# A gated mix of attention and MLP in split fp32: engine queues filled from a build-time plan instead of hand-written delays

## The chip, the core and the metric

The kernel runs on one core of one Trainium2 chip. A core has a matrix engine (TensorE, PE in the profile, with its weight loads as PEld), three engines that work on elements (VectorE, DVE; ScalarE, ACT; GpSimd, POOL) and SyncE (SP), whose queue issues the transfers here. Each engine works through a queue of its own strictly in order; which instruction stands where in a queue is fixed when the kernel is built. The metric is the device time of one execution in microseconds, lower is better.

## The reference

For 2,048 positions of 448 features:

```python
g = sigmoid((x * gate_w).sum(-1))
# a: 16 heads of 28; query s sees the keys s, s-2, ... s-14 (8 of them, none below 0)
q, k, v = split(x @ wqkv)
a = softmax(q . k[s - 2 w] * 28**-0.5) . v[s - 2 w], then @ wo
h = relu(x @ w1 + b1) ** 2                      # 448 -> 1792
b = h @ w2 + b2                                 # 1792 -> 448
out = g * a + (1 - g) * b
```

Everything is fp32.

## The kernel before

**Products in parts.** TensorE multiplies numbers in a reduced form (fp32r). Each operand is therefore split: ScalarE copies its *high* part to fp32r, and a subtraction gives the *low* part, mostly on VectorE (`split_full`, lines 115 and 116). A product is three matmuls: high by high, high by low, low by high. In the names of the trace a final `h` or `l` tells the part (`w2ah`, `w2al`). The feature size 448 is three slices of 128 rows and one of 64; the matmuls use 64 rows each, in *pairs*: one on the upper and one on the lower half of the array, for two accumulators side by side (`side_by_side`, line 184). Each accumulator has to see both halves, so at mid-way the two change places. Before that a tiny instruction must be put between (`turn`, lines 192 and 194: a write to an unused column of the accumulator, on VectorE but for one case; in the MLP a `touch`, line 527, that rewrites a few weights in place on ScalarE).

**Layout.** Since the attention steps by two, positions are ordered by parity (`par`), and x comes in four chunks of 512 columns, two for each parity.

**Stages on TensorE.** Phase A computes q, k, v for the chunks in turn (`qkv_first`, line 253, then `qkv_two`); ScalarE evacuates the accumulators to stage tiles (`st`, line 203), which are stored to DRAM (`q_d`, `k_d`, `v_d`, line 209). From there the attention runs without TensorE, in eight units (parity by four head groups): q and k or v are loaded (lines 301, 302, 307), GpSimd multiplies (line 325 q by k, line 332 weights by v, eight of each in a unit, 128x896 each), VectorE reduces each product (lines 326 and 340), softmax lies between (lines 363 to 378), and the output is transposed (line 343) and stored (`o_d`, line 353). The product tiles have four buffers.

Meanwhile TensorE runs the MLP: 28 rounds, four chunks in the order 3, 0, 1, 2 with 14 tiles of 128 hidden features in pairs of two. In a round come `h_first` (12 pairs of matmuls of 512 columns), the touch, the first half of the second layer for the round before (`o_part`, 12 pairs of 448 columns, `b<-w2ah,h` and the like), a touch, `h_second` (9 pairs), and the second half (`o_all`, 12 pairs). For each of a round's two hidden tiles `mlp_ops` issues relu with bias (line 576), the square as high part (line 577), the square in place (line 578), all on ScalarE, and on VectorE the low part (line 575). Below, "low" without more is this one. `o_part` reads the high parts first and the lows from its third pair on.

At a chunk's end VectorE forms the gated sum (`bt`, line 762). The product of the attention's output with `wo` (`a`) is done in eight units: four for the first parity are slipped in between the MLP's rounds, four stand at the end. Their input is loaded (`ot`, lines 813 and 815) and split (lines 832 to 836).

Weights of the second layer come in two groups: `w2a`, in pieces of four and three tiles (`w2_piece`, lines 511 to 515; the low parts of the first on VectorE, of the second on GpSimd), and `w2b`, tile by tile (`w2_first`, line 903, two lows on GpSimd; the other five by way of a copy to an accumulator, line 897, on VectorE).

**What sets the order.** TensorE's stream is written out. The other engines' instructions are placed between its matmuls by hand: `advance` moves a clock of TensorE's time, `at`, `soon` and `when` put a function into a list with a time of that clock (constants `LO_DELAY`, `HL_DELAY`, `SPLIT_GAP`, `ATT_DELAY` and others), and the attention is a generator that is drawn on as its own clock falls behind:

```python
    def at(dt, fn):
        later.append((clock["pe"] + dt, fn))
...
        while clock["att"] < clock["pe"]:
            try:
                r = next(att)
```

Of the kernel before, what the change touches and what calls it, by code (L numbers as in the profile page):

```python
# [7 lines left out]
F32 = mybir.dt.float32  # L8
# [6 lines left out]
P = 128  # L15
# [15 lines left out]
MM512 = 227.0  # L31
MM448 = 203.0
QK_COST = 2300.0
AV_COST = 2000.0
SM_COST = 600.0
ATT_DELAY = 20000.0
LO_DELAY = 1500.0
HL_DELAY = 1800.0
SPLIT_GAP = 2000.0
ROW_GAP = 9200.0  # L40
OUT_DELAY = 2500.0
OUT_GAP = 3500.0
WO_DELAY = 4500.0
LOAD_DELAY = 1500.0
LAND_DELAY = 5000.0
OL_DELAY = 2500.0
KEY_DELAY = 10500.0
DEFER = 2
# [5 lines left out]
BT_BUFS = 8  # L54


@with_exitstack
def gated_mix_kernel(ctx: ExitStack, tc: tile.TileContext, xT, wqkv, w1, w2, wo, b1, b2, out):
# [5 lines left out]

# [6 lines left out]


# [6 lines left out]

    w1h = const.tile([P, 3, F], F32R, name="w1h")  # L80
    w1l = const.tile([P, 3, F], F32R, name="w1l")

# [12 lines left out]

# [15 lines left out]
    def now(fn):  # L111
        fn()

    def split_full(raw, hi, lo, soon=now):
        nc.scalar.activation(hi, raw, AF.Copy)
        soon(lambda: nc.vector.tensor_sub(lo, raw, f32(hi)))  # L116

    def split_x78(raw, x7, x8, soon=now):

        split_full(raw, x7, x8, soon)  # L120

    class X:

        def __init__(self, tiles):
            self.t = tiles
            self.h, self.l = [t[:, 0] for t in tiles[:3]], [t[:, 1] for t in tiles[:3]]
            self.x7, self.x8 = tiles[3][:, 0], tiles[3][:, 1]

# [3 lines left out]
    def x_split(raw, x, k):  # L134

        split_full(raw[:, k], x.t[k][:, 0], x.t[k][:, 1])

    def x_spill(c, x):
        for j in range(4):
            nc.sync.dma_start(x_d[c, j], f32(x.t[j]))  # L140
# [4 lines left out]

# [5 lines left out]

# [7 lines left out]
    stage = {}  # L159

# [3 lines left out]
    def block(b):  # L164

        o = (0, NP, NP + D)[b]
        return slice(o, o + ncols(b))

    class Acc:


        def __init__(self, tag, name, n, todo=21):
            self.pt, self.n, self.todo, self.rows = ps(tag, name), n, todo, None
            self.all = todo

    def side_by_side(*todo):


        assert len(todo[0]) == len(todo[1])
        for pair in zip(*todo):  # L180
            for r, (acc, a, w) in enumerate(pair):
# [3 lines left out]
                acc.todo, acc.rows = acc.todo - 1, r  # L185

    def turn(one, two):


        for acc in (one, two) if one is not two else (one,):  # L190
            if one is two:
                nc.scalar.activation(acc.pt[0:1, 511:512], none, AF.Copy)
            else:
                nc.vector.memset(acc.pt[0:1, 511:512], 0.0)  # L194
            acc.rows = None

    def qkv_evacuate(pt, c, tl, b):
        par, t = c // 2, (c % 2) * 4 + tl
        first = (b, t // 2) not in stage
        if first:  # L200
            stage[b, t // 2] = xap.tile([P, G, 2, C], F32, tag="stage", name=f"st{c}_{tl}_{b}", bufs=ST_BUFS)
        st = stage[b, t // 2]
        nc.scalar.activation(st[:, :, t % 2], pt[:, :D].rearrange("p (g c) -> p g c", g=G), AF.Copy)  # L203
        if not first:
# [4 lines left out]
            nc.sync.dma_start(dd.rearrange("p g s c -> p g (s c)"), st.rearrange("p g s c -> p g (s c)"))  # L209
        if b == 0:  # L210
            nc.scalar.activation(zt[:, par, t:t + 1], pt[:, D:D + 1], AF.Copy)

    def full(x, acc, tl, b, ks=range(3)):
        sl, n = slice(tl * P, tl * P + P), block(b)
        r = []
        for k in ks:
            r += [(acc, x.h[k][:, sl], wqh[:, k, n]), (acc, x.h[k][:, sl], wql[:, k, n]),
                  (acc, x.l[k][:, sl], wqh[:, k, n])]
        return r

    def last(x, acc, tl, b):

# [3 lines left out]
        return [(acc, x.x7[:, sl], h), (acc, x.x7[:, sl], l), (acc, x.x8[:, sl], h)]  # L226
# [4 lines left out]
    def run(c, todo, steps):  # L231


        a = 0
        for e, done, *turns in steps:
            side_by_side(todo[0][a:e], todo[1][a:e])
            while a < e:
                advance(min(12, e - a) * MM448)
                a = min(a + 12, e)
            for t in turns:  # L240
                t() if callable(t) else turn(*t)
            for b, tl, acc in done:
                assert acc.todo == 0
                qkv_evacuate(acc.pt, c, tl, b)

    def qkv_first(x):

        four = range(4)
        q = accs(0, 0, four, "bbbb")
        for k in range(3):  # L250
            for i in four:
                for j, (acc, a, w) in enumerate(full(x, q[i], i, 0, (k,))):
                    nc.tensor.matmul(acc.pt[:, :NQ], a, w, start=k == j == 0, stop=False)  # L253
            advance(12 * MM448)
# [19 lines left out]

# [12 lines left out]
    o_t = {}  # L287
    st_ = {"spilled": -1, "att": -1}
# [9 lines left out]
    def att_load_qk(par, g):  # L298
        q = attp.tile([P, NS, C], F32, tag="q", name=f"q{par}{g}")
# [773 lines left out]
```

## Time and profile before

| | us |
|---|---|
| median of 3 runs | 425.17 (424.88, 425.17, 425.71) |
| span of the profiled execution | 423.9, 9,324 instructions; 1.3 below the median |
| PE busy | 411.2 (97%), 3,844 matmuls |
| VectorE, ScalarE, GpSimd busy | 262.1, 199.4, 271.3 |
| mean granted TensorE clock | 0.997 |

The span reaches from the first to the last instruction of one profiled execution. The runs' time also holds what lies around it; no separate time of the profiled execution is given, so its own time is taken as its span plus the 1.3 us by which the median lies above. In the timeline each row has its start, its length, the engine, line and operation, and how many instructions it holds; the bracket behind it is the idle time ahead of it on its engine, with what ended that.

### The profile page before, as it was taken

Reading aid. Unit: us, or ns where it says so; the run is one execution under the profiler, and the core shown is the slowest. Engines: PE = TensorE matmul, PEld = TensorE weight load, DVE = VectorE, ACT = ScalarE, POOL = GpSimd, SP = SyncE. Lnnn points to the kernel's source line nnn. Section 1 sums busy time; section 2 is a strip of 40 time slices with the busy share of each in tenths; the row PEclk is TensorE's granted clock in tenths of the full one; section 3 lists DMA queues with packets and bytes.
Section 4 is the critical chain, followed back from the end, with each engine's and each line's share of the span. In section 5 each row is a group of like instructions: output and inputs, shape, how many; then the busy total and the mean of one; then the engine's idle time right before and its main releaser. Section 6 shows DMA issues by size and latency. Waiting matters only on the chain.

```text
span 423.9 us, 9324 instructions
## 1 busy us (share of the span) xinstructions
PE 411.2 (97%) x3844; PEld 373.3 (88%) x3844; DVE 262.1 (62%) x400; ACT 199.4 (47%) x453; POOL 271.3 (64%) x170
## 2 busy tenths in 40 slices
PE   8999999899999799999999998999999999999995
PEld 6999999899988688888888887889988888888995
DVE  4520523773565766867675577798678477697353
ACT  3642555234656275444455533535461344446630
POOL 0000001940599999999899898889899879593000
PEclk9999999999999999999999999999999999999998
DMA  7999799937564050735310448883545420218804
GB/s 219 362 329 324 228 366 301 351 118 240 212 202 145 27 201 9 288 111 175 126 57 27 147 151 272 179 248 110 120 168 187 177 88 2 82 70 191 165 14 174
DMA packets 65323, 73.76 MB, mean 174 GB/s; under 512 B 32320, under 2 KB 58368, under 8 KB 64896
## 3 DMA queue, kind: packets, MB, share of 16 engines
q1 hardware_dynamic: 65280, 73.16, 52.9%
q8 instruction: 30, 0.49, 0.5%
q14 instruction: 13, 0.11, 0.1%
HBM read 45.71 MB, written 28.25 MB: 174 GB/s over the span
## 4 chain that ended last, share of the span: by engine, by line
PE 80%; POOL 7%; DMA 5%; DVE 4%; ACT 2%; SPq 1%; issue 1%; DVEq 0%; POOLq 0%; ACTq 0%
PE b L184 27%; PE h L184 26%; PE qkv L184 18%; PE a L184 8%; POOL qk L325 4%; DMA k<-k_d 2%; DVE w17l L116 2%; DMA ot<-o_d 2%; POOL av L332 1%; PE qkv L253 1%; DMA xraw<-xT 1%; POOL w2al L515 1%; DVE o L340 1%; POOL w2bl L903 1%; DVE h L575 0%
## 5 line engine op out<-in xcount | busy, mean ns | idle before, releaser
L325 POOL TENSOR_TENSOR qk<-q,k 128x896 f32<-128x896 f32 x64 | 135.2, 2135 | 103.5 <-DMA k<-k_d 89.9
L332 POOL TENSOR_TENSOR av<-lg,v 128x896 f32<-128x896 f32 x64 | 118.6, 1962 | 8.2 <-DMA v<-v_d 4.5
L184 PE MATMUL qkv<-wqh,x 64*128 64x448 f32 (+1 forms) x528 | 90.3, 362 | 1.5 <-DVE qkv L194 1.5
L575 DVE TENSOR_TENSOR h<-h,h 128x512 fp32r<-128x512 f32 x56 | 38.5, 687 | 56.8 <-ACT h L578 56.4
L326 DVE TENSOR_REDUCE lg<-qk 128x32 f32<-128x896 f32 x64 | 67.5, 1075 | 8.6 <-POOL qk L325 8.6
L184 PE MATMUL b<-w2ah,h 64*128 64x448 f32 x448 | 67.0, 362 | 4.9 <-DVE h L575 4.9
L184 PEld LDWEIGHTS qkv<-wqh,x 64*128 64x128 f32 x528 | 69.8, 184 | 2.1 <-DVE qkv L194 1.9
L340 DVE TENSOR_REDUCE o<-av 128x112 f32<-128x896 f32 x64 | 66.9, 1072 | 6.3 <-POOL av L332 6.1
L184 PE MATMUL qkv<-wql,x 64*128 64x448 f32 (+1 forms) x264 | 68.4, 362 | 0.0
L184 PE MATMUL b<-w2bh,h 64*128 64x448 f32 x448 | 66.6, 360 | 0.0
L576 ACT ACTIVATE h<-h,b1z 128x512 f32<-128x512 f32 x56 | 36.7, 656 | 40.6 <-PE h L184 40.6
L184 PEld LDWEIGHTS b<-w2ah,h 64*128 64x128 f32 x448 | 41.6, 184 | 10.1 <-DVE h L575 6.4
L184 PEld LDWEIGHTS b<-w2bh,h 64*128 64x128 f32 x448 | 41.9, 184 | 3.9 <-ACT h L527 0.3
L203 ACT ACTIVATE st<-qkv 128x448 f32<-128x448 f32 x48 | 24.6, 542 | 42.2 <-PE qkv L184 35.7
L184 PE MATMUL b<-w2al,h 64*128 64x448 f32 x224 | 40.7, 359 | 0.0
L184 PEld LDWEIGHTS qkv<-wql,x 64*128 64x128 f32 x264 | 40.4, 184 | 0.1
L184 PE MATMUL b<-w2bl,h 64*128 64x448 f32 x224 | 40.5, 358 | 0.0
L577 ACT ACTIVATE h<-h 128x512 fp32r<-128x512 f32 x56 | 33.5, 599 | 2.0 <-POOL lg L363 0.4
L578 ACT ACTIVATE h<-h 128x512 f32<-128x512 f32 x56 | 33.2, 594 | 0.0
L184 PE MATMUL h<-x,w1h 64*128 64x512 f32 x168 | 29.3, 387 | 0.0
L184 PE MATMUL h<-x1b,w1h 64*128 64x512 f32 x168 | 28.3, 388 | 0.3 <-ACT w1h L527 0.3
L527 ACT ACTIVATE h<-h 128x4 fp32r<-128x4 f32 (+1 forms) x32 | 6.6, 206 | 46.5 <-PE b L184 46.5
(125 smaller groups left out, 700.5 us busy)
## 6 DMA issues: line engine op xcount, KB each, us to landing
k<-k_d SPq DMA_DIRECT2D x8, 840.0 KB, 5.2
v<-v_d SPq DMA_DIRECT2D x8, 840.0 KB, 5.1
x_d<-x SPq DMA_DIRECT2D x12, 512.0 KB, 5.4
q_d<-st SPq DMA_DIRECT2D x8, 448.0 KB, 2.7
k_d<-st SPq DMA_DIRECT2D x8, 448.0 KB, 3.7
v_d<-st SPq DMA_DIRECT2D x8, 448.0 KB, 4.2
w1raw<-w SPq DMA_DIRECT2D x4, 896.0 KB, 8.7
q<-q_d SPq DMA_DIRECT2D x8, 448.0 KB, 3.3
```

Source lines behind the costliest of these rows:

```text
L116: soon(lambda: nc.vector.tensor_sub(lo, raw, f32(hi)))
L184: nc.tensor.matmul(acc.pt[:, :acc.n], a[rows], w[rows], start=acc.todo == acc.all, stop=acc.todo == 1)
L203: nc.scalar.activation(st[:, :, t % 2], pt[:, :D].rearrange("p (g c) -> p g c", g=G), AF.Copy)
L325: nc.gpsimd.tensor_mul(pr, q[:, s:s + 1].to_broadcast([P, W, C]), k[:, s:s + W])
L326: pending.append(lambda: nc.vector.tensor_reduce(lg[:, s], pr.rearrange("p w (h d) -> p w h d", h=HG), axis=AX.X, op=ALU.add))
L332: nc.gpsimd.tensor_mul(pr.rearrange("p (h d) w -> p w h d", h=HG), lg[:, s][:, :, :, None].to_broadcast([P, W, HG, DH]), v[:, s:s + W].rea ...
L340: nc.vector.tensor_reduce(o[:, g * C:(g + 1) * C], pr, axis=AX.X, op=ALU.add)
L527: nc.scalar.activation(ap, f32(ap), AF.Copy)
L575: nc.vector.tensor_sub(hl, pt, f32(hh))
L576: ops += [lambda pt=pt, r=r: nc.scalar.activation(pt, pt, AF.Relu, bias=b1t[:, f + r:f + r + 1]), lambda pt=pt, hh=hh: nc.scalar.activatio ...
L577: lambda pt=pt, hh=hh: nc.scalar.activation(hh, pt, AF.Square),
L578: lambda pt=pt, r=r, low=low: (nc.scalar.activation(pt, pt, AF.Square), at(delays[r], low))]
```

## The change

The delays, the lists and the generator go. Every instruction outside TensorE's stream becomes a *job* with an engine, an assumed duration, the jobs it needs and an urgency (`TURN` first, then `NEXT`, `SOON`, `MID`, `LATE`, `LAST`). A `Plan` keeps a clock for each engine while the kernel is built: `pe` moves TensorE's clock by a pair, `need` moves it on to the end of a job that the next matmul reads, and `step` takes, of all engines, the job that could start first, or a more urgent one that can start within 600 ns. So the order in each queue comes out of the assumed durations. The plan also keeps room for urgent work (`hold`), spaces transfers (`wire`, `BACKLOG`, `calm`), and lets no subtraction from two SBUF tiles on VectorE start while a product on GpSimd is assumed to run (`port`). Nothing of the plan exists at run time. Accumulators and stage tiles are handed out by a `Ring`.

What differs in the queues, besides order:

- The turns of phase A are all on ScalarE.
- The attention's output tiles have a pool of their own (`heads_out`, eight buffers); before they shared the pool `bp`.
- The low parts of the second `w2a` piece and of `w2b` go to VectorE; a `w2a` piece is one instruction (128x1792 and 128x1344) instead of one a tile; four `w2b` lows are subtracted straight from SBUF, three by way of an accumulator. The low parts of three `w1` slices are one instruction.
- TensorE's stream has the same matmuls in the same order, but the `wo` units of the first parity come one round earlier.
- x chunks are split and put aside earlier in phase A, and in SP's queue one `w2a` load and the q and k loads of the second attention unit stand ahead of the last stores of phase A.

Instructions in the queues go from 434 to 481 on ScalarE, 385 to 342 on VectorE, 173 to 170 on GpSimd and 183 to 191 on SP.

```diff
-ATT_DELAY = 20000.0
-LO_DELAY = 1500.0
-HL_DELAY = 1800.0
-SPLIT_GAP = 2000.0
...
+HOLD = 600.0
+BACKLOG = 3000.0
+TURN, NEXT, SOON, MID, LATE, LAST = range(6)
...
+    def begin(self, j):
+        r = max(j.at, self.free[j.eng])
+        for d in j.deps:
+            e = self.end(d)
+            if e is None:
+                return None
+            r = max(r, e + LAT)
+        if j.prio > NEXT and r < self.hold[j.eng] < r + j.cost:
+            r = self.hold[j.eng]
+        if j.move and j.prio >= MID:
+            r = max(r, self.wire - BACKLOG)
+        if j.move and j.prio > NEXT:
+            if r < self.calm < max(r + j.cost + 1250.0, self.wire) + j.move[0] * (8.0 + j.move[1] / 25.2) / 16 - 1250.0:
+                r = self.calm
+        return max(r, self.port) if j.port else r
+    def step(self, limit):
+        best = None
+        for eng, jobs in self.jobs.items():
+            can = [(s, j) for j in jobs if (s := self.begin(j)) is not None]
+            if not can:
+                continue
+            first = min(s for s, _ in can)
+            s, j = min(((s, j) for s, j in can if s <= first + (HOLD if j.prio <= NEXT else 1.0)),
+                       key=lambda x: (x[1].prio, x[1].n))
+            if best is None or s < best[0]:
+                best = (s, j)
+        if best is None or best[0] > limit:
+            return False
+        s, j = best
+        self.jobs[j.eng].remove(j)
+        self.now = max(self.now, s)
+        j.start = s
+        if j.move:
+            packets, size = j.move
+            self.free[SYNC] = s + j.cost + 45.0
+            self.wire = max(s + j.cost + 1250.0, self.wire) + packets * (8.0 + size / 25.2) / 16
+            j.done = self.wire + 450.0
+        else:
+            j.done = s + j.cost
+            self.free[j.eng] = j.done - {ACT: 10.0, DVE: 80.0, POOL: 55.0, SYNC: 0.0}[j.eng]
+            if j.port:
+                self.port = j.done - 120.0
+        j.fn()
+        return True
+    def need(self, *jobs):
+        for j in jobs:
+            while self.end(j) is None:
+                assert self.step(float("inf")), "nothing to do"
+            self.t = max(self.t, j.done + LAT)
+        self.run()
+    def pe(self, cost):
+        self.t += cost
+        self.run()
...
-    opool = bp
+    opool = ctx.enter_context(tc.tile_pool(name="heads_out", bufs=1))
...
     def side_by_side(*todo):
         assert len(todo[0]) == len(todo[1])
         for pair in zip(*todo):
-            for r, (acc, a, w) in enumerate(pair):
+            need(*(j for e in pair for j in (*e[0].after, *e[3:])))
+            for r, (acc, a, w, *_) in enumerate(pair):
                 rows = slice(r * 64, r * 64 + 64)
                 assert acc.rows in (None, r)
                 nc.tensor.matmul(acc.pt[:, :acc.n], a[rows], w[rows], start=acc.todo == acc.all, stop=acc.todo == 1)
-                acc.todo, acc.rows = acc.todo - 1, r
+                acc.todo, acc.rows, acc.after = acc.todo - 1, r, ()
+            plan.pe(MM512 if pair[0][0].n == CH else MM448 + (pair[0][0].n - D) * 1.7)
     def turn(one, two):
         for acc in (one, two) if one is not two else (one,):
-            if one is two:
-                nc.scalar.activation(acc.pt[0:1, 511:512], none, AF.Copy)
-            else:
-                nc.vector.memset(acc.pt[0:1, 511:512], 0.0)
+            acc.after = (add(ACT, 200.0, lambda acc=acc: nc.scalar.activation(acc.pt[0:1, 511:512], none, AF.Copy),
+                             plan.after_pe(), prio=TURN),)
             acc.rows = None
...
-    def advance(dt):
-        clock["pe"] += dt
-        for item in sorted([x for x in later if x[0] <= clock["pe"]], key=lambda x: x[0]):
-            later.remove(item)
-            item[1]()
-        if not clock["on"]:
-            clock["att"] = clock["pe"]
-            return
-        while clock["att"] < clock["pe"]:
-            try:
-                r = next(att)
-            except StopIteration:
-                clock["on"] = False
-                return
-            if r is None:
-                clock["att"] = clock["pe"]
-                return
-            clock["att"] += r
-    def go(todo, cost):
-        n = len(todo[0])
-        for a in range(0, n, 3):
-            side_by_side(todo[0][a:a + 3], todo[1][a:a + 3])
-            advance(min(3, n - a) * cost)
+    def go(todo):
+        side_by_side(*todo)
...
-    def w2_piece(i0, n, t, gap, eng):
-        raw = raw_tile(f"w2raw{i0}")
-        nc.sync.dma_start(raw[:, :n, :D], w2[:, i0:i0 + n])
-        def part(k):
-            nc.scalar.activation(w2ah[:, i0 + k], raw[:, k, :D], AF.Copy)
-            soon(lambda: eng.tensor_sub(w2al[:, i0 + k], raw[:, k, :D], f32(w2ah[:, i0 + k])))
-        for k in range(n):
-            when(t + k * gap, part, k)
+    def w2_piece(i0, n, buf, *deps):
+        hold, got = raw_load(buf, f"w2raw{i0}", w2[:, i0:i0 + n], lambda r: r[:, :n, :D], 128 * n, 1792, *deps, prio=MID)
+        js = []
+        his = [add(ACT, cost_act(D), lambda k=k: nc.scalar.activation(w2ah[:, i0 + k], hold[0][:, k, :D], AF.Copy), got,
+                   prio=LATE) for k in range(n)]
+        low = add(DVE, cost_dve(n * D), lambda: nc.vector.tensor_sub(
+            w2al[:, i0:i0 + n], hold[0][:, :n, :D], f32(w2ah[:, i0:i0 + n])), *his, prio=LATE, port=True)
+        for k, h in enumerate(his):
+            w2_jobs[i0 + k] = (h, low)
+        js += [*his, low]
+        raw_free[hold[1]] = js
...
-    def mlp_ops(accs, c, f, delays):
-        h = rawp.tile([P, 4, CH], F32R, tag="raw", name=f"h{c}_{f}")
-        ops = []
-        for r in range(2):
-            pt, hh, hl = accs[r].pt, h[:, 2 * r], h[:, 2 * r + 1]
-            def low(hl=hl, pt=pt, hh=hh):
-                nc.vector.tensor_sub(hl, pt, f32(hh))
-            ops += [lambda pt=pt, r=r: nc.scalar.activation(pt, pt, AF.Relu, bias=b1t[:, f + r:f + r + 1]),
-                    lambda pt=pt, hh=hh: nc.scalar.activation(hh, pt, AF.Square),
-                    lambda pt=pt, r=r, low=low: (nc.scalar.activation(pt, pt, AF.Square), at(delays[r], low))]
-            hs[c, f + r] = (hh, hl)
-        return ops
+    def mlp_ops(accs, c, f):
+        need(*h_ring.pop(0))
+        h = rawp.tile([P, 4, CH], F32R, tag="raw", name=f"h{c}_{f}")
+        ready = plan.after_pe()
+        for r in range(2):
+            pt, hh, hl = accs[r].pt, h[:, 2 * r], h[:, 2 * r + 1]
+            a = add(ACT, 656.0, lambda pt=pt, r=r: nc.scalar.activation(pt, pt, AF.Relu, bias=b1t[:, f + r:f + r + 1]),
+                    ready, bias_job[0], prio=NEXT)
+            b = add(ACT, 600.0, lambda pt=pt, hh=hh: nc.scalar.activation(hh, pt, AF.Square), a, prio=NEXT)
+            a = add(ACT, 600.0, lambda pt=pt: nc.scalar.activation(pt, pt, AF.Square), b, prio=NEXT)
+            low = add(DVE, 690.0, lambda pt=pt, hh=hh, hl=hl: nc.vector.tensor_sub(hl, pt, f32(hh)), a, prio=NEXT)
+            hs[c, f + r] = (hh, hl, b, low)
+            accs[r].ring.give(low)
...
-    def w2_first(f):
-        raw, (hi, lo) = row_raw(f"w2raw{f}", w2[:, f]), w2hl(f)
-        at(6500.0, lambda: nc.scalar.activation(hi, raw, AF.Copy))
-        at(8500.0, lambda: nc.gpsimd.tensor_sub(lo, raw, f32(hi)))
+        h = add(ACT, 563.0, lambda: nc.scalar.activation(hi, hold[0], AF.Copy), js[-1], prio=LATE)
+        if direct:
+            low = add(DVE, 620.0, lambda: nc.vector.tensor_sub(lo, hold[0], f32(hi)), h, prio=SOON, port=True)
+        w2_jobs[f] = (row(name, w2[:, f], *w2hl(f), direct=f < NFA + 4), row_low[name])
```

1031 lines of the change are left out of this document (585 added, 446 removed).

## Prediction

> **What bounds the kernel now.** I read the page first, for the engine that is busy and for its clock; then the waits of TensorE; then TensorE's timeline at each wait, and the queue of the engine that it waited for.
>
> ```profile
> span 423.9 us, 9324 instructions
> PE 411.2 (97%) x3844; PEld 373.3 (88%) x3844; DVE 262.1 (62%) x400; ACT 199.4 (47%) x453; POOL 271.3 (64%) x170
> PEclk9999999999999999999999999999999999999998
> ```
>
> TensorE is busy for 97% of the span, at the full clock until the last slice. The change leaves its 3,844 matmuls as they are, so it can win only what lies between them. The waits view lists that completely:
>
> ```profile
> PE b L184 <- DVE h L575: 4.9, 3, 2.6
> PE qkv L184 <- DVE qkv L194: 1.5, 1, 1.5
> PE warm L587 <- DVE zero L585: 1.2, 1, 1.2
> PE h L184 <- ACT w1h L527: 0.3, 1, 0.3
> PE qkv L253 <- DVE x L612: 0.2, 1, 0.2
> ```
>
> The third and fifth belong to the start (warm-up, first x) and are not touched. The others are five stalls, 4.9 + 1.5 + 0.3 = 6.7 us of idle time. TensorE's timeline shows what each costs; the bracket is the idle time ahead of the instruction and its releaser:
>
> ```profile
> 78.89 0.48 PE L184 MATMUL qkv<-wqh,x 64*128 64x448 f32 x2 [1.51 <-DVE qkv L194]
> ...
> 120.84 0.64 PE L184 MATMUL b<-w2ah,h 64*128 64x448 f32 x4
> 121.24 0.43 PE L184 MATMUL b<-w2al,h 64*128 64x448 f32 x2
> 122.62 0.68 PE L184 MATMUL b<-w2ah,h 64*128 64x448 f32 x4 [0.94 <-DVE h L575]
> ...
> 142.64 0.68 PE L184 MATMUL b<-w2ah,h 64*128 64x448 f32 x4 [2.59 <-DVE h L575]
> ...
> 257.49 0.36 PE L184 MATMUL b<-w2al,h 64*128 64x448 f32 x2
> 259.20 0.67 PE L184 MATMUL b<-w2ah,h 64*128 64x448 f32 x4 [1.35 <-DVE h L575]
> 259.71 0.37 PE L184 MATMUL b<-w2al,h 64*128 64x448 f32 x2
> ...
> 270.80 0.49 PE L184 MATMUL h<-x1b,w1h 64*128 64x512 f32 x2 [0.27 <-ACT w1h L527]
> ```
>
> Undisturbed, a pair of 448 columns follows the last after 0.20 us. At 257 the next pair was due at 257.49 + 0.20 = 257.69 and came at 259.20; its two pairs took 0.51 instead of 0.40. The loss is 1.51 + 0.11 = 1.62 us, against 1.35 shown as idle: a stop costs its idle time plus about 0.28, since the overlap of neighbours is lost as well. Five stops: 6.66 + 5 x 0.28 = 8.0 us. Without them the span would be 423.9 - 8.0 = 415.9 us. That is the most the change can gain, apart from the two ends.
>
> **The change part by part.** *Turns of the row halves go from VectorE to ScalarE.* The stall at 77 is a tiny write that stood behind large work:
>
> ```profile
> L116 DVE TENSOR_TENSOR w17l<-w1raw,w17h x16: 216/286/2220, 50.0 to 100.3; 64x128 fp32r<-64x128 f32 x12, 64x64 fp32r<-64x64 f32 x4
> 71.96 6.79 DVE L116 TENSOR_TENSOR w17l<-w1raw,w17h 64x64 fp32r<-64x64 f32 x4 [1.38 <-ACT w17h L115]
> 78.76 0.06 DVE L194 MEMSET qkv<- 1x1 f32 x3
> 111.19 2.14 POOL L325 TENSOR_TENSOR qk<-q,k 128x896 f32<-128x896 f32 x1 [19.00 <-DMA k<-k_d]
> ```
>
> Four subtractions of 64x64 took 6.79 us, up to 2.22 each where the median is 0.286. A GpSimd product lasts 2.14, and those subtractions fell into its first unit: VectorE waited out one product per subtraction, and the turn, queued last, waited for all. The GPSIMD Engine Reference of the Trainium skill (section "8. Key points") says that GpSimd shares its SBUF interfaces with VectorE, with contention for VectorE instructions with two SBUF inputs. By that rule the change is worse elsewhere, for it moves more such subtractions to VectorE (below); the trace agrees, by the 2.22 against 0.286.
>
> On ScalarE a turn costs more itself:
>
> ```profile
> L192 ACT ACTIVATE qkv<-b1z x2: 163/163/163, 14.7 to 15.4; 1x1 f32<-1x1 f32 x2
> 24.65 2.19 ACT L115 ACTIVATE x<-xraw 128x512 fp32r<-128x512 f32 x4
> 30.43 0.98 ACT L203 ACTIVATE st<-qkv 128x448 f32<-128x448 f32 x2 [3.59 <-PE qkv L184]
> ```
>
> 0.16 us against 0.06, behind at most one copy (2.19 / 4, some 0.55). A turned accumulator is used nine pairs later, 9 x 0.20 = 1.8 us. So the stall at 77 goes, 1.51 + 0.28 = 1.8, and the turns are hidden. In one place they are not safe: around 77 two turns stand right behind the copy of a just-loaded w1 piece in ScalarE's new queue; a load 4 us late would bring a wait back.
>
> The same queue has one visible flaw. Around 31 us the high part of a k-slice of the third x chunk now stands ahead of the evacuations that begin at 30.43. It overwrites a tile that TensorE reads until about 31, so it starts then, and the evacuation some 0.6 to 1 us later than before; the freed bank is what the next chunk begins with. Bounds 0 (the bank is not needed at once) and 1.0 (the whole delay arrives); I take 0.3, nearer the first, since only the first of four accumulators is so tight.
>
> *h's low parts get their place on VectorE by urgency.* The three stalls on line 575 have one pattern:
>
> ```profile
> 140.90 1.09 DVE L340 TENSOR_REDUCE o<-av 128x112 f32<-128x896 f32 x1 [0.66 <-POOL av L332]
> 141.90 0.68 DVE L575 TENSOR_TENSOR h<-h,h 128x512 fp32r<-128x512 f32 x1
> ...
> 254.76 2.07 DVE L340 TENSOR_REDUCE o<-av 128x112 f32<-128x896 f32 x2
> 256.75 1.27 DVE L762 SCALAR_TENSOR_TENSOR bt<-b,zg,bt 128x448 f32<-128x448 f32 x2
> 257.93 0.64 DVE L343 STREAM_TRANSPOSE o<-o 128x448 f32<-128x448 f32 x1
> 258.49 0.65 DVE L575 TENSOR_TENSOR h<-h,h 128x512 fp32r<-128x512 f32 x1
> ```
>
> At 141 the second low part stood behind two reductions that themselves waited for GpSimd; at 258 behind two reductions, two adds and a transpose, 2.07 + 1.27 + 0.64 = 4.0 us of work that nobody on TensorE needed. At 122 it was one reduction. In the new queue each low stands behind no more than one reduction or one add that could still be running, so 4.9 us of idle and 3 x 0.28, 5.7 in all, go. What is late next is the first low of a round. In the round of 121 its last input on ScalarE came from here:
>
> ```profile
> 118.03 0.59 ACT L578 ACTIVATE h<-h 128x512 f32<-128x512 f32 x1
> ```
>
> That ends at 118.62, and the first pair that reads the low is in the row at 120.84, the first that reads the second low was due at 121.24 + 0.20 = 121.44. So the first has 2.2 us, needs 0.68 itself, and bears one reduction of 1.09 ahead of it with 0.45 left.
>
> Against this, VectorE takes over the low parts of w2 from GpSimd:
>
> ```profile
> L515 DVE TENSOR_TENSOR w2al<-w2raw,w2ah 128x448 fp32r<-128x448 f32 x4 | 2.3, 620 | 3.6 <-ACT w2ah L514 3.6
> L515 POOL TENSOR_TENSOR w2al<-w2raw,w2ah 128x448 fp32r<-128x448 f32 x3 | 3.4, 1168 | 0.0
> L903 POOL TENSOR_TENSOR w2bl<-w2raw,w2bh 128x448 fp32r<-128x448 f32 x2 | 2.3, 1144 | 0.0
> ```
>
> GpSimd loses 3.4 + 2.3 = 5.7 us, VectorE gains 5 x 0.62 = 3.1, both with room (64% and 62% busy). The seven w2al rows become two wide instructions in phase A, where no h is due. Four w2bl rows are now subtracted straight from SBUF, and there the port counts: each may wait for a product's end, 0 to 2.14 us, and one of them stands with a reduction right ahead of a first low, that of the MLP's third round; behind the others no low follows closely. Bounds: 0 (it is through before the square ends) and 2.14 + 0.62 + 1.09 + 0.68 - 2.2 = 2.3 (all of it begins when the square ends). I take 0.5, nearer the first: the reduction behind it waits for the same product, so that the subtraction's wait overlaps it. By the rule of the Trainium skill named above (GPSIMD Engine Reference, "8. Key points") the subtraction would wait in full, and the sum would be 418.5 + 1.8 = 420.3 us.
>
> *The attention runs earlier.* Between its first two units GpSimd stood idle for 19.0 us (row above), for this:
>
> ```profile
> 86.28 0.46 SPq L209 DMA_DIRECT2D v_d<-st  x1
> ...
> 99.77 2.23 SPq L511 DMA_DIRECT2D w2raw<-w  x2
> ...
> 102.72 8.31 DMA k<-k_d
> ```
>
> The key load stood in SP's queue behind three stores of phase A and both w2 loads, which need the buffers that phase A's end frees. In the new queue one w2 load and the q and k loads stand ahead of those stores: they follow the store at 86.28, so I estimate the issue at 86.28 + 0.46 + 2.23 = 89 and the products, with the same 8.31, near 97 instead of 111.2. TensorE did not wait for GpSimd there, so this gains nothing directly; it gives every later reduction, and wo's inputs, some 14 us of lead. It is the cover on which the low parts' new places rest.
>
> *wo's units come one round earlier, output tiles have their own place.* At 270 the loads and copies of an attention output stood ahead of the touch that TensorE needed:
>
> ```profile
> 268.58 0.85 ACT L832 ACTIVATE oh<-ot 128x768 fp32r<-128x768 f32 x1 [2.10 <-DMA ot<-o_d]
> 270.55 0.19 ACT L527 ACTIVATE w1h<-w1h 128x2 fp32r<-128x2 f32 x1
> ```
>
> The queue position of this load is now about 15 us ahead of its use with the attention's lead, so this stop goes (-0.3 - 0.28). Since the unit is needed a round sooner, a little of the lead is spent. For such small stops, of the class 0.27 shown here, over the 28 rounds I add 0.5: two of them; none and four (1.1) are the bounds.
>
> *Ends.* TensorE's order at the start is kept, and the tail is an add and a store behind the last matmul in both kernels: 0 for each.
>
> **Sum.** 423.9 - 8.0 + 0.3 + 0.5 + 0.5 = 417.2 us of span. The profiled execution's own time is not told apart from the runs; the median 425.17 is 1.3 above the span, and I carry that: 418.5 us, with 415.9 + 1.3 = 417.2 and 415.9 + 1.0 + 2.3 + 1.1 + 1.3 = 421.6 as bounds of the unknown terms.
>
> **The rivals.** *Stops move, not vanish* (partly). ScalarE and VectorE are strict queues; one order fixed at build time is right only if loads, products and contention run as assumed. Places: the turns at 77 behind the w1 copy, the w2bl rows, chunk ends where adds and lows alternate. Each wrong place costs what the old ones cost, 0.6 to 2.9 us. Three of them of 1.6 beyond the sum: 423.3 us. For it: the old stops came from exactly this, and VectorE gets more port-bound work. Against: reading the queues, I find at most one reduction ahead of each low. *Nothing happens*: the old order was as good and the stops are set by GpSimd's speed: 425 us. Against it: at 258 the low waited for VectorE alone.
>
> *Slower.* GpSimd runs late against the order written into VectorE's queue. In the MLP's first round the second low now stands behind the sixth reduction of the second attention unit. TensorE needs that low at about 121.44 - 1.8 + 0.3 = 119.9 (when it was due before, less the removed stop, plus the flaw at 31). If the products start at S, the low is there at S + 6 x 2.14 + 1.09 + 0.68 = S + 14.6. It decides from S = 105.3. Near 97 there are 8 us in hand; with S = 111.2, as before, TensorE loses 5.9 us, and 418.5 + 5.9 = 424.4. To be slower S must pass 112.8; at 115 (the loads held until phase A's last buffers are free, and sharing their DMA time with two w2 loads) it is 418.5 + 9.7 = 428.2 us. For it: 8.31 us for a key load beside two w2 loads. Against: in the new order only one w2 load stands ahead of the keys.
>
> **How the numbers follow.** Forecast (418.5, within 417.2 to 421.6): 0.68. Stops move (423.3): 0.13, all still faster. Nothing happens: 0.05. Slower: 0.14, with what I can't see in it. A measurement of this kernel tells 0.2% (0.85 us) from no change; so faster 0.81, same 0.05, slower 0.14. The range of 8 in 10 runs from 416.8 (no stop at all, 417.2, and 0.4 for the spread of the runs) to 423.5, which takes in the rival whose stops move.
>
> **What would show it.** In the waits of TensorE after, lines for the turn, for h's low parts and for the touch together below 1.5 us; GpSimd's idle time before its second unit about 5 us instead of 19.0; products starting near 97; the w2bl subtractions on VectorE at up to 2 us each; TensorE's busy time again 411. Wrong would be a wait of TensorE on h's low above 2 us in the first two rounds (slower rival), a row of waits of 0.5 to 3 us on ScalarE or on h (stops move), or a TensorE wait on anything that DMA releases.

## The result and the profile after

The changed kernel takes 417.81 us (median of four runs, 417.22 to 419.09) against 425.44 for the kernel before beside it; the ratio is 0.9839 with an interval of 0.9802 to 0.9876. Forecast were 418.5 us and a range of 416.8 to 423.5.

The page of the changed kernel, its span and its busy times, and then the whole of its waits view for TensorE (total, times, longest):

```profile
span 417.3 us, 9285 instructions
PE 410.8 (98%) x3844; PEld 375.6 (90%) x3844; DVE 265.5 (64%) x348; ACT 202.8 (49%) x495; POOL 272.1 (65%) x165
```

```profile
PE warm L736 <- DVE zero L734: 1.2, 1, 1.2
PE qkv L393 <- DVE x L759: 0.4, 1, 0.4
```

All five stops are gone and no new one is listed; what is left belongs to the start. The view leaves out very short waits, so small losses have to be read from the times of the matmuls (three of them below). This profile was of the run of 419.09 us, the slowest, and has a start of its own: the full pace of TensorE came 5 us late (last section). A second profile of the same kernel (e9 below, span 415.4) starts nearly as the kernel before does, so its timeline can be laid beside the rows of the prediction, at the same matmuls of the stream. The first two rows are of the kernel before, where the pairs begin and, behind the moved `wo` units, where both kernels have again done the same matmuls; the rest are of the second profile:

```profile
13.79 0.47 PE L184 MATMUL qkv<-w7h,x 64*128 64x450 f32 x2
...
320.87 0.39 PE L184 MATMUL h<-x1b,w17h 64*128 64x512 f32 x2
```

```profile
13.45 0.47 PE L309 MATMUL qkv<-w7h,x 64*128 64x450 f32 x2
...
77.12 0.44 PE L309 MATMUL qkv<-wql,x 64*128 64x448 f32 x2
...
119.48 0.60 PE L309 MATMUL b<-w2ah,h 64*128 64x448 f32 x4
...
136.64 0.68 PE L309 MATMUL b<-w2ah,h 64*128 64x448 f32 x4
...
251.50 0.56 PE L309 MATMUL b<-w2ah,h 64*128 64x448 f32 x4
...
312.38 0.39 PE L309 MATMUL h<-x1b,w17h 64*128 64x512 f32 x2
```

| stop | before, at | second profile | lead | gained here | forecast (idle + 0.28) |
|---|---|---|---|---|---|
| start of the pairs | 13.79 | 13.45 | 0.34 | 0.34 | 0 |
| turn at 77 | 79.20 | 77.12 | 2.08 | 1.74 | 1.79 |
| low at 122 | 122.62 | 119.51 | 3.11 | 1.03 | 1.22 |
| low at 142 | 142.64 | 136.64 | 6.00 | 2.89 | 2.87 |
| low at 259 | 259.20 | 251.50 | 7.70 | 1.70 | 1.63 |
| touch at 270, and all up to 320 | 320.87 | 312.38 | 8.49 | 0.79 | 0.55 |

(A row that holds four matmuls starts with the first; 119.51 is the third of the row at 119.48. What is gained at a stop is the growth of the lead since the row above, so small losses in between are in it.) The five add up to 8.15 us where 8.0 were forecast.

### The profile page after: what moved, and what is told of

Same layout as the page of the kernel before. It is cut to its first block, busy times and chain, and to the rows that moved or that the text cites. A ratio compares the mean times of both kernels' runs of the same rounds, so it can differ in the third digit from the quotient of the medians.

```text
span 417.3 us, 9285 instructions
## 1 busy us (share of the span) xinstructions
PE 410.8 (98%) x3844; PEld 375.6 (90%) x3844; DVE 265.5 (64%) x348; ACT 202.8 (49%) x495; POOL 272.1 (65%) x165
## 4 chain that ended last, share of the span: by engine, by line
PE 96%; DVE 1%; DMA 1%; ACT 0%; DVEq 0%; issue 0%; SPq 0%
PE b L309 31%; PE h L309 31%; PE qkv L309 23%; PE a L309 8%; PE qkv L393 2%; DMA xraw<-xT 1%; DVE w2bl L1076 0%; DVE h L724 0%; DVE o L517 0%; DVE bt_b L950 0%; ACT h L720 0%; ACT h L722 0%; DVEq L1249 0%; PE warm L396 0%; ACT h L723 0%
## 5 line engine op out<-in xcount | busy, mean ns | idle before, releaser
L497 POOL TENSOR_TENSOR pp<-q,k 128x896 f32<-128x896 f32 x64 | 140.8, 2235 | 85.9 <-DMA k<-k_d 80.5
L509 POOL TENSOR_TENSOR pp<-lg,v 128x896 f32<-128x896 f32 x64 | 119.7, 1973 | 4.5 <-DVE lg L501 4.3
L309 PE MATMUL qkv<-wqh,x 64*128 64x448 f32 (+1 forms) x528 | 89.3, 362 | 0.0
L501 DVE TENSOR_REDUCE lg<-pp 128x32 f32<-128x896 f32 x64 | 67.8, 1077 | 9.2 <-POOL pp L497 9.1
L517 DVE TENSOR_REDUCE o<-pp 128x112 f32<-128x896 f32 x64 | 67.2, 1068 | 4.5 <-POOL pp L509 4.4
L309 PE MATMUL qkv<-wql,x 64*128 64x448 f32 (+1 forms) x264 | 65.2, 362 | 0.0
L309 PEld LDWEIGHTS qkv<-wql,x 64*128 64x128 f32 x264 | 39.3, 184 | 0.1
L667 ACT ACTIVATE w1h<-w1h 128x2 fp32r<-128x2 f32 x28 | 5.8, 207 | 57.6 <-PE h L309 57.6
L309 PE MATMUL h<-x0b,w1h 64*128 64x512 f32 x168 | 28.1, 386 | 0.0
```

The costliest lines, as they stand in the source:

```text
L309: nc.tensor.matmul(acc.pt[:, :acc.n], a[rows], w[rows], start=acc.todo == acc.all, stop=acc.todo == 1)
L497: nc.gpsimd.tensor_mul(pr.rearrange("p (w c) -> p w c", w=W), q[:, s:s + 1].to_broadcast([P, W, C]), k[:, s:s + W])
L501: nc.vector.tensor_reduce(lgs[i][:, s], pr.rearrange("p (w h d) -> p w h d", w=W, h=HG), axis=AX.X, op=ALU.add)
L509: nc.gpsimd.tensor_mul(pr.rearrange("p (h d w) -> p w h d", h=HG, w=W), lgs[i][:, s][:, :, :, None].to_broadcast([P, W, HG, DH]), vs[i][:, ...
L517: nc.vector.tensor_reduce(o_t[par, s][:, g * C:(g + 1) * C], pr.rearrange("p (c w) -> p c w", w=W), axis=AX.X, op=ALU.add)
L667: return add(ACT, 205.0, lambda: nc.scalar.activation(ap, f32(ap), AF.Copy), *deps, prio=TURN)
```

## The experiments

The times are medians, the ratios against the kernel before, run beside it (425.0 to 425.2 us).

**e1, turns alone, in the kernel before.**

```diff
-            if one is two:
-                nc.scalar.activation(acc.pt[0:1, 511:512], none, AF.Copy)
-            else:
-                nc.vector.memset(acc.pt[0:1, 511:512], 0.0)
+            nc.scalar.activation(acc.pt[0:1, 511:512], none, AF.Copy)
```

> The kernel before, with all turns of phase A as ScalarE writes and nothing else changed. Theory (each stop of TensorE is a place in a strict queue, and is worth its idle time plus about 0.28 us): the stop at 77 us goes and nothing takes its place, for ScalarE's last work ahead of that turn ended at 72.3 us; 425.4 - 1.8 = 423.6 us, the other four stops stay as they were. Rival (the subtractions under GpSimd's products hold TensorE by another way, or the turn waits on ScalarE instead): a wait of 1 to 2 us at the same place, 425 us.

423.90 us, ratio 0.9980 (0.9963 to 0.9998). The turn's wait is gone, the lows' are as before:

```profile
PE b L184 <- DVE h L572: 4.7, 3, 2.6
```

So the turn's engine matters, by itself. The gain is 1.2 us and not 1.8. A part of that is chance: the stop at 77 isn't in every execution of the old queue (e2). In this profile TensorE gains 2.0 us at 77 against the same matmuls before, but loses 0.4 near 104, where a turn now stands behind the copy of a late w2a load on ScalarE, and 1.3 at 140, where the clock is halved behind the stop (last section).

**e2, lows alone, in the kernel before: both queued at once.**

```diff
-        ops = mlp_ops(accs, c, f, (HL_DELAY, HL_DELAY if ends else 2 * HL_DELAY))
+        ops = mlp_ops(accs, c, f, (0.0, 0.0))
```

(and so in the two other calls)

> The kernel before, with the delays of h's low parts set to zero, so that each round's two low parts are queued on VectorE together and ahead of the reductions of that time, save in the first round, where the second stays behind two reductions of the late second attention unit. Theory (place alone): the stops of 2.59 us at 142 and 1.35 us at 259 go, the one of 0.94 us at 122 stays, and the turn's too: 425.4 - 2.59 - 1.35 - 0.56 = 420.9 us. Rival (VectorE, held by low parts that wait for ScalarE, does the reductions late, GpSimd waits for its buffers, and TensorE stops later for the attention's output): those two stops go but the one at 270 grows by 1 us or more; 422 to 426 us.

429.84 us, ratio 1.0129 (1.0093 to 1.0165): slower, and both theories missed. The stops at 142 and 259 on the lows went, but at each chunk's end something else came late. VectorE's and the weight loads' timeline at one:

```profile
184.85 0.69 DVE L575 TENSOR_TENSOR h<-h,h 128x512 fp32r<-128x512 f32 x1 [3.53 <-ACT h L578]
186.54 0.69 DVE L575 TENSOR_TENSOR h<-h,h 128x512 fp32r<-128x512 f32 x1 [1.00 <-ACT h L578]
187.15 1.27 DVE L762 SCALAR_TENSOR_TENSOR bt<-b,zg,bt 128x448 f32<-128x448 f32 x2
```

```profile
190.06 0.18 PEld L184 LDWEIGHTS b<-w2ah,h 64*128 64x128 f32 x1 [0.48 <-DVE bt L762]
```

VectorE stood 4.5 us for its two lows, and the gated sums, which free the accumulators of the next chunk, were queued behind them. TensorE lost about 1.3 us at 190 and again at 347 against the same matmuls before, and about 2.6 at 260, where the clock was halved as well (last section); three late lows near 147 to 150 cost 2.6, and late loads of x near 177 and 334 some 1.6. A low must be neither too late nor too early in the queue.

The same run shows the turn of 77 from another side. The keys of the first unit came 1.3 us later than in the profile of before, so no product ran beside the four subtractions, and in the same queue there was no stop:

```profile
71.87 1.28 DVE L116 TENSOR_TENSOR w17l<-w1raw,w17h 64x64 fp32r<-64x64 f32 x4 [1.09 <-ACT w17h L115]
...
73.58 4.21 POOL L325 TENSOR_TENSOR qk<-q,k 128x896 f32<-128x896 f32 x2 [72.19 <-DMA k<-k_d]
```

1.28 us for the four, against 6.79 beside products.

**e3, both of these edits.**

> The two edits of the first two runs together in the kernel before. Theory: the gains add, 425.4 - 1.8 - 4.5 = 419.1 us; against the changed kernel's 417.8 there remain the stop at 122 (1.2) and the one at 270 (0.6), with their 0.28 each counted. Rival (the plan as a whole is needed, and single places only move the waits): 422 us or more.

429.23 us, ratio 1.0100 (1.0082 to 1.0117). The rival held: single places, moved by a rule that is the same in each round, only move the waits.

**e4, turns back on VectorE in the changed kernel**, placed by the plan.

```diff
-            acc.after = (add(ACT, 200.0, lambda acc=acc: nc.scalar.activation(acc.pt[0:1, 511:512], none, AF.Copy),
+            acc.after = (add(DVE, 60.0, lambda acc=acc: nc.vector.memset(acc.pt[0:1, 511:512], 0.0),
```

> The changed kernel with the turns of phase A back on VectorE as small memsets, placed there by the plan with the same urgency and a duration of 60 ns. Theory (the engine matters, since a memset queued behind a subtraction under a product waits for it, whatever the plan assumes): a stop of TensorE on the turn near 77 to 79 us of 0.5 to 2.5 us; 418.4 to 420.5 us. Rival (the plan alone, which keeps subtractions off running products, finds a place on VectorE too): no stop, 417.8 us.

420.41 us, ratio 0.9895 (0.9876 to 0.9914): 2.6 above the changed kernel. The theory held in size, not in place; at 79 only 0.23 us of idle time are left, the large stop is here (TensorE, then VectorE):

```profile
105.25 0.47 PE L309 MATMUL qkv<-wqh,x 64*128 64x448 f32 x2 [1.79 <-DVE qkv L316]
```

```profile
102.29 2.82 DVE L639 TENSOR_TENSOR w2al<-w2raw,w2ah 128x1344 fp32r<-128x1344 f32 x1 [2.66 <-ACT w2ah L637]
105.05 1.07 DVE L501 TENSOR_REDUCE lg<-pp 128x32 f32<-128x896 f32 x1
105.12 0.06 DVE L316 MEMSET qkv<- 1x1 f32 x2
```

The turn stood behind the wide subtraction of w2a, which came late and ran long beside products.

**e5, urgency of the lows**, one word of the plan.

```diff
-            low = add(DVE, 690.0, lambda ...: nc.vector.tensor_sub(hl, pt, f32(hh)), a, prio=NEXT)
+            low = add(DVE, 690.0, lambda ...: nc.vector.tensor_sub(hl, pt, f32(hh)), a, prio=LATE)
```

> The changed kernel with one urgency altered: h's low parts are LATE instead of NEXT, so that reductions that can start at the same time go ahead of them in VectorE's queue; the same matmuls in the same order. Theory (the urgency of the lows is what took the stops on them away): the second low of the first round now stands behind the seventh reduction and two small steps and comes about 0.4 us late, and others follow; TensorE's waits list h's low parts again, 1 to 5 us in all, 419 to 423 us. Rival (the earlier attention gives the lead by itself, the urgency adds nothing): no wait on them, 417.8 us.

423.09 us, ratio 0.9959 (0.9945 to 0.9974). The wait is back at the size that it had before:

```profile
PE b L309 <- DVE h L724: 5.2, 6, 1.3
```

5.3 us of the gain are this urgency: the largest part of the change.

**e6, a plan that is wrong about GpSimd.**

```diff
-            return product(2130.0, mul, red, got["q", i], got["k", i], *lg_use.get(i - 2, ()))
+            return product(1700.0, mul, red, got["q", i], got["k", i], *lg_use.get(i - 2, ()))
...
-            j = product(1955.0, mul, red, got["v", i])
+            j = product(1560.0, mul, red, got["v", i])
```

> The changed kernel whose plan is told that GpSimd's products last 1.70 and 1.56 us instead of 2.13 and 1.96; the chip does them as before. In VectorE's queue the first round's first low then stands behind all eight reductions of the second unit and the first of the next product kind. Theory (GpSimd late against the order written into VectorE's queue stops TensorE, the prediction's slower rival): that low is ready at about 101.1 + 8 x 2.3 + 2 + 2 + 1.1 + 0.7 = 125.3 where TensorE needs it at 120.6, a stop of some 5 us, and smaller ones later; 423 to 430 us. Rival (TensorE's slack and the four product buffers absorb it): below 419.5 us.

456.87 us, ratio 1.0755 (1.0728 to 1.0782), 39 us above the changed kernel and far past the theory's range:

```profile
PE a L309 <- DVE o L1029: 11.3, 2, 8.6
PE b L309 <- DVE h L724: 11.0, 13, 1.2
```

The first low was 1 us late, not 5, but GpSimd falls further behind the plan with each unit: thirteen stops on lows, and two where a `wo` unit stands in TensorE's stream ahead of its attention output (8.6 us at 295). About 26 us of idle time in all; the rest is refilling and half clock after the longer stops (last section).

**e7, keys late without the plan's knowledge.**

```diff
+NDUM = 8
...
+                for r in range(NDUM if i == 1 else 0):
+                    nc.sync.dma_start(dum[r], x_d[0, r % 4])
                 nc.sync.dma_start(qk[i][1], halo_ap(k_d, par, g))
```

> The changed kernel with the same order in every queue, but eight extra copies of 0.5 MB from DRAM to DRAM are issued ahead of the key load of the second attention unit; the plan does not know of them. They take bandwidth and SP's queue and make the keys late, by 8 to 20 us. Theory (the prediction's slower rival: the second low of the first round stands behind the sixth reduction): the products start at S instead of 101.1; TensorE loses S - 104 us or so, 424 to 431 us for S from 110 to 117, all of it in one stop on h's low part in the first round or two, and little after. Rival (something else waits first, a store of phase A or the x of the next chunk): the stops are on other releasers.

432.43 us, ratio 1.0179 (1.0152 to 1.0205). Dearer than forecast, and the rival's case: the products started at 112.1 us, for which the theory's S - 104 gives 8 us; the time is 14.6 above the changed kernel, and the stop is a turn's. GpSimd, TensorE, ScalarE and SP:

```profile
112.09 7.51 POOL L501 TENSOR_TENSOR pp<-q,k 128x896 f32<-128x896 f32 x3 [22.13 <-DMA k<-k_d]
```

```profile
115.38 0.74 PE L311 MATMUL qkv<-wqh,x 64*128 64x448 f32 x2 [12.67 <-ACT qkv L318]
```

```profile
113.68 1.51 ACT L641 ACTIVATE w2ah<-w2raw 128x448 fp32r<-128x448 f32 x3 [14.98 <-DMA w2raw<-w]
115.09 0.61 ACT L318 ACTIVATE qkv<-b1z 1x1 f32<-1x1 f32 x6
```

```profile
91.03 5.45 SPq L464 DMA_DIRECT2D dum<-x_d  x8
98.82 0.34 SPq L465 DMA_DIRECT2D k<-k_d  x1
100.55 0.39 SPq L609 DMA_DIRECT2D w2raw<-w  x1
```

The second w2a load, behind the keys, came late too, and the copies of it stand ahead of six turns in ScalarE's queue. The trace has TensorE at half clock until 121.4: of the 14.6 us, 12.7 are idle time, and most of the rest comes of 6.0 us at half clock. No wait on a low is left: held there, TensorE needed the lows later as well.

**e8, w2's low parts back on GpSimd** (seven instructions of 1.15 us).

```diff
-            low = add(DVE, 620.0, lambda: nc.vector.tensor_sub(lo, hold[0], f32(hi)), h, prio=SOON, port=True)
+            low = add(POOL, 1145.0, lambda: nc.gpsimd.tensor_sub(lo, hold[0], f32(hi)), h, prio=SOON)
```

(and the second `w2a` piece, tile by tile)

> The changed kernel with the low parts of the second w2a piece and of four w2b tiles back on GpSimd (three and four instructions of 1.15 us), the plan knowing it. Theory (which engine has them matters little, since the plan makes room on either): no stop above 0.3 us, 417.3 to 418.6 us. Rival A (the port, by the prediction's weighed rule: VectorE's four subtractions cost up to 2.3 us): faster than 417.3. Rival B (GpSimd, later by 7 x 1.15 = 8 us, makes the reductions and with them h's lows late): 419 to 423 us.

419.42 us, ratio 0.9867 (0.9830 to 0.9903): by the number the second rival's case, by the waits not, for no low is waited for. The only stop is a turn behind the copy of the last w1 piece:

```profile
PE qkv L309 <- ACT qkv L316: 1.1, 2, 0.9
```

That place has nothing to do with the edit (e9, e10). So the move of w2's lows is worth little, and its sign isn't settled.

**e9, the changed kernel again.** **e10, the last w1 piece's copies behind those turns.**

> The changed kernel unaltered, for more of its runs and a second profile. In its first profile the full clock came only at 10 us and TensorE was 1.3 us late from there on. Theory (a chance of the start: x arrived 0.4 us late): here the full clock comes near 5 us, the span is 415.5 to 416.5, and, TensorE being earlier against the loads, the turns behind the copy of the last w1 piece stop it by 0 to 1.2 us near 77; 417.0 to 418.2 us. Rival (the change itself moved the start): the full clock again near 10 us.

```diff
+        at = 78500.0 if i == 2 else 0.0
...
-        his = [add(ACT, cost_act(n), lambda k=k: nc.scalar.activation(...), got, prio=LATE) for k in range(3)]
+        his = [add(ACT, cost_act(n), lambda k=k: nc.scalar.activation(...), got, prio=LATE, at=at) for k in range(3)]
```

(and the same `at` for the rest of the piece, `w17`)

> The changed kernel, with the plan told that the copies and subtractions of the w1 piece that is loaded last cannot start before 78.5 us of its clock; so the two turns that stood behind the first of its copies on ScalarE go ahead of it. Theory (these turns are the only place left that waits for a load): no wait of TensorE on a turn, whenever the piece lands; 0 to 1 us faster than the changed kernel beside it, 416.8 to 417.6 us. Rival (the pieces' low parts then come late for the first hidden tile, or the delay moves a stop to VectorE's subtractions): a wait on w1 or h, 418 us or more.

e9 took 417.39 us, ratio 0.9826 (0.9809 to 0.9843), with the full pace from the start and a span of 415.4, 0.1 below its theory's range: the theory held. The piece landed in time in that profile. e10 took 416.70, ratio 0.9809 (0.9792 to 0.9826), a little below its theory's range. ScalarE in e10:

```profile
72.80 0.32 ACT L316 ACTIVATE qkv<-b1z 1x1 f32<-1x1 f32 x2
76.11 1.05 ACT L614 ACTIVATE w1h<-w1raw 128x448 fp32r<-128x448 f32 x2 [2.99 <-DMA w1raw<-w]
```

The two turns no longer wait for the piece. It is the fastest version of all: four runs of 416.52 to 417.15 beside 417.15 to 417.98 of e9. The intervals overlap, so the 0.7 us are likely rather than shown. Nor do the two profiles show them at these turns: TensorE passes there at 77.12 us in e9 and at 77.09 in e10.

**e11, a plan that knows nothing of the port.**

```diff
-        return max(r, self.port) if j.port else r
+        return r
```

> The changed kernel with a plan that takes no account of the port: subtractions on VectorE from two SBUF tiles are placed as if they ran at full speed beside GpSimd's products. Theory (on the chip they wait for a product's end, up to 2.1 us each, as w17l did): lows or turns queued behind them come late, 0.5 to 4 us of stops; 418.3 to 422 us. Rival (the lows' slack of 1 to 2 us covers it): within 0.5 us of the changed kernel.

429.10 us, ratio 1.0102 (1.0085 to 1.0120): worse than the theory, by another way. VectorE, SP, ScalarE and TensorE:

```profile
86.76 3.81 DVE L240 TENSOR_TENSOR w17l<-w1raw,w17h 64x128 fp32r<-64x128 f32 x4
```

```profile
90.60 0.37 SPq L605 DMA_DIRECT2D w2raw<-w  x1
```

```profile
95.97 1.97 ACT L637 ACTIVATE w2ah<-w2raw 128x448 fp32r<-128x448 f32 x4 [8.51 <-DMA w2raw<-w]
97.85 0.61 ACT L316 ACTIVATE qkv<-b1z 1x1 f32<-1x1 f32 x6
```

```profile
98.14 0.74 PE L309 MATMUL qkv<-wqh,x 64*128 64x448 f32 x2 [8.01 <-ACT qkv L316]
```

The subtractions beside products ended at 90.57; only then was their buffer free for the w2a load, which the plan took to be earlier and whose copies it had put ahead of six turns. Lows cost 0.7 us only.

**e12, output tiles back in `bp`**, all queues unchanged.

```diff
-    opool = ctx.enter_context(tc.tile_pool(name="heads_out", bufs=1))
+    opool = bp
```

> The changed kernel with the attention's output tiles back in the pool bp, which reuses the memory of phase A; every queue has the same instructions in the same order. Theory (place costs nothing here: bp is free before the first output is written near 124 us): the same time within 0.5 us. Rival (the first outputs wait for the last readers of phase A's tiles, so that VectorE's queue and the lows in it are late): a stop on h's low part near 122 us, 418.5 to 420 us.

417.45 us, ratio 0.9829 (0.9810 to 0.9847), beside 417.39 for e9: the place is worth nothing.

## Why the prediction was right, step by step

**The bound and the price of a stop** held: 8.15 us for the five, by the table, against 8.0. Shown are the lows (e5 brings 5.2 us of them back) and the turn's engine (e1, e4). That the two must come with a plan for each round was not in the prediction's sum; e2 and e3 show it.

**The three additions came at about half of their 1.3 us**, too short for the waits view, which the prediction took to be complete. At 31 the flaw is there (ScalarE, second profile): the copy of x stands ahead of the evacuation, which starts at 31.18 instead of 30.43 and ends at 31.71.

```profile
30.64 0.63 ACT L239 ACTIVATE x<-xraw 128x512 fp32r<-128x512 f32 x1 [0.74 <-PE qkv L309]
31.18 0.53 ACT L331 ACTIVATE st<-qkv 128x448 f32<-128x448 f32 x1
```

The matmul that waits for it starts at 31.76, and from there TensorE's lead over the kernel before is 0.1 to 0.2 us smaller: 0.1 to 0.2 for 0.3. The w2b place was named rightly; the subtractions ran up to 2.08 us, and the first low of the third round came late by this (tile view, weight loads and TensorE of the changed kernel):

```profile
L1076 DVE TENSOR_TENSOR w2bl<-w2raw,w2bh x4: 906/1332/2077, 131.2 to 142.0; 128x448 fp32r<-128x448 f32 x4
```

```profile
138.50 0.30 PEld L309 LDWEIGHTS b<-w2ah,h 64*128 64x128 f32 x4 [0.44 <-DVE h L724]
```

```profile
138.04 0.38 PE L309 MATMUL b<-w2al,h 64*128 64x448 f32 x2
138.50 0.68 PE L309 MATMUL b<-w2ah,h 64*128 64x448 f32 x4
139.01 0.36 PE L309 MATMUL b<-w2al,h 64*128 64x448 f32 x2
```

Three pairs took 139.01 - 138.04 = 0.97 us instead of 0.60: 0.4 for 0.5, and 0.2 in the second profile. The subtractions contend with products, as the Trainium skill (GPSIMD Engine Reference, "8. Key points") has it for VectorE instructions with two SBUF inputs; the trace agrees, by 0.91 to 2.08 us where 0.62 is the time alone. That section gives no length for the wait; the 420.3 us that the prediction drew from it needed all of the wait to reach TensorE, and at most 0.4 did. Of small stops there is one of 0.2 us near 103, at a turn, for 0.5; in e8 and e12 the turn behind the w1 copy cost 0.7 to 1.1, the unsafe place that the prediction had named.

**The offset** was mis-sized: the first profile is of the 419.09 run with a span of 417.3, 1.8 apart and not 1.3. The two middle runs have spans of 415.9 and 416.1 where 417.2 were forecast. In the second profile, at 415.4, some 0.7 of the missing 1.8 us are the additions that came short; the rest is 0.34 at the start and small gains between the stops, which the sum did not have. That 418.5 lies so near 417.81 is in part luck: 1.2 us too much in the span and 0.5 too little in the offset have opposite signs.

**The earlier attention** came, less than forecast (GpSimd and SP, changed kernel):

```profile
101.11 8.78 POOL L497 TENSOR_TENSOR pp<-q,k 128x896 f32<-128x896 f32 x3 [9.47 <-DMA k<-k_d]
```

```profile
91.74 0.37 SPq L605 DMA_DIRECT2D w2raw<-w  x1
...
92.71 0.63 SPq L461 DMA_DIRECT2D k<-k_d  x1
```

101.1 for 97, an idle time of 9.5 for 5: the w2a load ahead of the keys waited until 91.7 for its buffer.

**The rivals.** "Stops move" is what e2, e3 and e11 did, not the change. The slower rival has the direction right (input that is late without the plan's knowledge stops TensorE) and price and place wrong: for products at 112.1 us its rule gives 112.1 - 105.3 = 6.8 us where e7 lost 14.6, and the first to give way is a turn behind a w2a copy on ScalarE, not the low behind the sixth reduction. No run takes back the earlier loads of the keys or the earlier `wo` units by themselves, so their share of the gain is not shown.

## What to carry to other kernels

Where strict queues feed one bound engine, price each stop by its releaser's queue: what stands ahead of the releasing instruction, and what that waits for. Place urgent small work by a model of every engine instead of one fixed delay, for a fixed delay that mends two places breaks others (e2). Such a plan is as good as its durations: 20% off on one engine cost 39 us (e6), so measure them under the contention in which they run, and don't put what TensorE needs next behind a copy that waits for a load.

## What the runs showed of the hardware

TensorE's pace halves at times. At the start it was slow for 5 us longer in the first profile of the changed kernel than in the second, over the same stretch (windows view: length, then the busy time and instructions of TensorE, its weight loads, VectorE, ScalarE and GpSimd; the third column from the end is the granted clock, which reads 1.00 here because these traces hold no clock before its first change, at 10.06 and at 4.80 us):

```profile
4.80:9.80 5.00, 4.99 (x14) 4.34 (x15) 3.53 (x8) 1.58 (x3) 0.00 (x0) 1.00 0.93 284
```

```profile
4.80:9.80 5.00, 4.87 (x22) 3.54 (x22) 2.45 (x7) 1.58 (x3) 0.00 (x0) 1.00 0.97 297
```

14 matmuls against 22; it cost 1.7 us. In the other thirteen profiles the full clock comes between 4.1 and 7.2 us. That the first profile's was later because x came 0.4 us late after the warm-up is likely, but not shown. And stops can bring it: in e1, after the stop of 2.57 us at 140:

```profile
136.50:139.92 3.42, 1.30 (x14) 0.85 (x10) 2.66 (x4) 1.24 (x4) 3.42 (x4) 1.00 0.00 0
...
140.00:143.20 3.20, 2.83 (x16) 2.55 (x18) 2.95 (x5) 0.00 (x0) 3.20 (x3) 0.50 0.00 0
143.20:146.40 3.20, 3.20 (x32) 2.73 (x30) 1.59 (x2) 1.47 (x4) 3.20 (x3) 0.98 0.01 3
```

In the profile of before, 2.59 us of idle time at the same place left the clock at 1.00:

```profile
138.21:141.62 3.41, 1.84 (x18) 1.29 (x14) 2.63 (x4) 1.24 (x4) 3.41 (x4) 1.00 0.09 32
```

In e2 a stop of 1.10 was enough:

```profile
260.40:263.80 3.40, 3.40 (x20) 3.02 (x20) 3.06 (x5) 0.21 (x1) 2.99 (x2) 0.50 0.99 282
```

Which stops bring it can be read from the traces. In all fourteen, every change of the clock comes a whole number of stretches of 3.41 us after its first rise: in e1 at 139.93, 39 of them after 6.81, in e2 at 260.43, 75 after 4.43. Between the start and the end of the program the clock fell eight times, each time behind a stretch in which TensorE had started 12 matmuls or fewer (10 in e1, 12 in e2; undisturbed it starts some 34), and it never fell behind one with 13 or more (14 in before, 13 in e3). Of e1's stop, 2.1 us lay in one stretch; that of before was cut by a boundary at 141.62 into 1.6 and 1.0. This is read off these traces, with a margin of a single matmul.

The Trainium skill (TensorE: Matmul & The Clock Gate, Part 1) has a free-running window of about 3.4 us and half rate after an idle one. The 3.41 us agree; that a whole window must be idle does not. So a stop's price is about 0.28 us above its idle time, and up to 1.7 more for each stretch that TensorE then runs at half clock. Where the stretches lie differs from run to run (the first rise, above), and so can the price of one and the same stop.
